# A fused attention and gated-MLP gradient kernel: DMA transfers moved between stretches, kv and W' blocks reordered, products of ones at the start, five residual sums moved to VectorE

## The chip, the cores and the metric

The kernel runs on one core of one Trainium2 chip. The metric is the device time of one execution in microseconds (us), here the median of several runs. The engines are called by their names or by those of the profile: TensorE (PE, its weight loads PEld), VectorE (DVE), ScalarE (ACT), GpSimd (POOL) and SyncE (SP), whose queue only issues DMA transfers. ScalarE and GpSimd can issue DMA transfers too.

## What is computed

The forward pass of a pre-LayerNorm block and its gradients for six of its inputs, with S = 2048 rows, D = 640, H = 32 heads of 20, F = 1728, in bf16:

```python
def A(x, wqkv, wo):                      # linear attention
    q, k, v = split_heads(x @ wqkv)
    phi = lambda t: where(t > 0, t + 1, exp(t)) + 1e-6
    pq, pk = phi(q), phi(k)
    kv = einsum("bhsd,bhse->bhde", pk, v)
    z = einsum("bhsd->bhd", pk)
    o = einsum("bhqd,bhde->bhqe", pq, kv) / (einsum("bhqd,bhd->bhq", pq, z)[..., None] + 1e-6)
    return merge_heads(o) @ wo
def B(x, w1, w3, w2):                    # gated MLP
    return (silu(x @ w1) * (x @ w3)) @ w2
h   = x + A(layernorm(x), wqkv, wo)
out = h + B(layernorm(h), w1, w3, w2)    # and the gradients for x, wqkv, wo, w1, w3, w2 from grad_out
```

## The kernel before

S is cut into 16 tiles of 128 rows (ST) or 4 chunks of 512 columns (SC), D into 5 blocks of 128 (DT), F into 14 (FT, the last of 64). Weights and activations stay in SBUF in pools that are stacked and reused; what does not fit is stored to DRAM scratch tensors (names in `_d`: pq_d, r_d, pk_d, xn_d, m_d, wT_d, kvT_d, hn_d, hh_d, gg_d) and loaded again for the backward part. The program is written in a manual schedule: the order of the calls in the source is the order of the instructions on each engine, and each engine, and each DMA-issuing queue, takes its own in that order. A wait of one instruction holds everything behind it on its engine or queue. The changes touch the forward part, which is the first 300 us or so.

**Start and k (lines 112 to 480).** x comes tile by tile, wqkv in column groups of 320 (`load_wq`, L176), both on SyncE's queue (`dma`). LayerNorm 1 takes two `BATCH_NORM_STATS` of half a row each (`Stats.part`, L147), an aggregate (L150), an addition (L151), a power on GpSimd (L152) and a normalisation (L155, on ScalarE for some tiles). For tiles 0 to 7 TensorE transposes the normalised rows (`p1_tr`, L246) and ScalarE copies them out of PSUM (L248), later tiles are transposed by DMA (L239). Then come the k products (`p1_mm`, L252), Exp and Relu on ScalarE (L269, L270) and two VectorE operations for phi (L273, L274). `m_part` accumulates M = pk^T xn for 5 row blocks (L382). The column sums of pk, Z, come along for the first blocks, `z_late` makes the rest. A list `trickle` of weight loads is issued one per tile. `ghh_chunk` (L361, L371) multiplies w2 (transposed by DMA, w2T) with a chunk of grad_out (transposed by DMA, g2T, two buffers) ahead of its use; the DMA transposes of w2T are cut in column ranges (L410), g2T is made per 512 rows (L216).

**q and M (lines 480 to 548).** q tiles (`q_tile`), the last row blocks of M with `m_end` (copies to mbs, and a DMA transpose to mT, L394), kvT blocks 0 and 1 (`kvT_block`: products at L401, then a masked copy by VectorE into bd, L203). For rows of pq the denominators are made in four steps: `r_prod` (product with Zb, on GpSimd for tiles below 6, L333), `r_red` and `r_inv` (L340 to L344), `r_scale` (L347), and `r_T`, a DMA transpose into pqT (L351).

**Hand-over (the list in `run`, lines 752 to 759).** PSUM is then shared by tags: "mm" with 4 banks, "o2" and "at" with 2 each. A step of the list is a function and its arguments: `q_late` (q tiles 10 to 15, L574, L575), `f2_mT` (the last block of mT by TensorE, L601), `f2_kv` (kvT blocks 2 to 4), `f2_wT` (W' = kv wo, L586, copied by ScalarE and VectorE to pkx, L589, and transposed by DMA to Wp, L590), then `f2_half` or `f2_at`, the residual: at = pq' Wp (L558). Where `on_pe` is true, x itself is added in PSUM by a product with the identity (L556) and ScalarE copies the sum back into x (L561). Otherwise VectorE adds x to PSUM (L563). LayerNorm 2 follows (`f2_hn`, `f2_ht`: transposes on TensorE, L633, in the first chunk). GpSimd's queue stores intermediate results: `q_out` to pq_d (L606), `f2_m_out` to m_d (L596), `r4_out` (L609), `r4b_out` (L612) and `r_out` (L355) to r_d, `f2_w_out` to wT_d (L593).

**MLP (lines 793 to 850).** For each of 4 chunks c and 14 column blocks fc: a ghh product four blocks ahead, the gate product (L361 by way of `mm5`), two sigmoids and a copy on ScalarE (L661 to L663), the up product and its copy (L669). Two blocks make a pair: VectorE runs 7 products and sums of it (L697), and three results are stored to hh_d and gg_d from SyncE's queue (L680). The tiles sig, s2, gate and up have 2 buffers, so a pair's copies wait until the stores of the pair two back have landed. `run_side` puts the residual and LayerNorm of the next chunk between, `r_steps` the denominators of tiles 6 to 15, which load pq back (`r_load`, L616), and `o2_steps` the down product of the chunk before (L721), which needs w2.

**Backward.** The rest (lines 860 to 1360) is untouched: long runs of products for the weight gradients and the input gradients.

Of the kernel before, what the change touches and what calls it, by code (L numbers as in the profile page):

```python
# [9 lines left out]
P = 128  # L10
# [45 lines left out]
def kernel(  # L56
# [116 lines left out]
    wqkv = U1.tile([P, DT, 3 * D], BF16, name="wqkv", tag="D")  # L173
    wq_v = A_wqkv.rearrange("(c p) n -> p c n", p=P)

    def load_wq(a, b):  # L176
        dma(out=wqkv[:, :, a * HD:b * HD], in_=wq_v[:, :, a * HD:b * HD])

    def load_x(a, b):
        dma(out=x_sb[:, a:b, :], in_=xS[:, a:b, :])  # L180

    load_wq(2, 3)
    load_x(1, 2)
    load_wq(3, 4)
    load_x(2, 4)
    load_x(4, 8)

    mask = cp.tile([P, DT, M_MAX, DH], BF16, name="mask")

# [38 lines left out]
    Z = cp.tile([P, DT], F32, name="Z")  # L228

    XT_DMA = 8  # L230

    def on_act(t):
        return t > XT_DMA and t % 2 == 0
# [178 lines left out]
    trickle = []  # L412

    zero_pads()
    load_g2T(0)
    load_x(8, 12)
    load_w2T(0, 2 * P)
    load_wq(0, 2)
    load_x(12, ST)
    ln1.run(x_sb, 0, 1)  # L420
    for a, b in ((0, 2 * P), (2 * P, D)):
        ln1.norm(x_sb[:, 0, a:b], x_sb[:, 0, a:b], 0)
    p1_tr(0, ((0, 2), (2, DT)))
    ln1.run(x_sb, 1, 2)
    ln1.run(x_sb, 2, 3)
    p1_norm(1)
    ln1.run(x_sb, 3, 4)
    p1_norm(2)
    trickle += [lambda: load_w2T(2 * P, 4 * P), lambda: load_wq(4, 6)]
    for c0, c1 in ((0, 2), (2, 4), (4, 5)):  # L430
        trickle += load_w13(c0, c1)
# [65 lines left out]
    q_tile(5)  # L497
    m_part(2, range(8, ST))
    m_end(2)
    phi_rest()  # L500
    m_part(3, range(5))
    z_row((2, 3, 4), big())
# [15 lines left out]
    r_prod(2)  # L518
    m_end(3)
    dmaG(out=m_v[:, 0:4, :], in_=mbs[:])  # L520
    load_w2T(8 * P, F)
    m_part(4, range(5))
    q_tile(8)
    kvT_block(1, big())
# [7 lines left out]
    q_tile(9)  # L532
    m_part(4, range(11, ST))
    m_end(4)
    phi_rest()
    r_scale(2)
    r_T(2)
    r_red(3)
    r_inv(3)
    r_prod(4)  # L540
    ps.release()
    load_x(0, 4)
    while trickle:
        trickle.pop(0)()

# [2 lines left out]
    hn, hnT, hhT = {}, {}, {}  # L548

    def f2_at(t, tag="at", halves=(0, 1)):  # L550
        on_pe = t < 2 * TPC
        for j in halves:
            at = ps.tile([P, 512], F32, name="at", tag=tag, bufs=2)
            xs = x_sb[:, t, j * HD:(j + 1) * HD]
            if on_pe:
                T.matmul(at[:, 0:HD], lhsT=ident[:], rhs=xs, start=True, stop=False)  # L556
            for c in range(DT):
                T.matmul(at[:, 0:HD], lhsT=pqT[:, c, t * P:(t + 1) * P], rhs=Wp[:, c, j * HD:(j + 1) * HD],  # L558
                         start=(c == 0 and not on_pe), stop=(c == DT - 1))
            if on_pe:  # L560
                A.copy(out=xs, in_=at[:, 0:HD])  # L561
            else:
                V.tensor_tensor(out=xs, in0=at[:, 0:HD], in1=xs, op=ALU.add)  # L563
            ln2.part(x_sb, t, j)

    def q_late(t):

        mq, rq = (p1.tile([P, D], BF16, name=n, bufs=b) for n, b in (("mq", 3), ("rq", 3)))
        q_home(t)
        for j in range(2):  # L570
            acc = ps.tile([P, 512], F32, name="mm", bufs=4)
            js = slice(j * HD, (j + 1) * HD)
            p1_half(acc[:, 0:HD], t, j * HD)
            A.activation(mq[:, js], acc[:, 0:HD], AF.Exp)  # L574
            A.activation(rq[:, js], acc[:, 0:HD], AF.Relu)  # L575

        def rest():
            V.tensor_scalar(out=mq[:], in0=mq[:], scalar1=1.0, scalar2=1e-6, op0=ALU.min, op1=ALU.add)
            V.tensor_tensor(out=pqs[t], in0=mq[:], in1=rq[:], op=ALU.add)  # L579
        held.append(rest)  # L580
# [15 lines left out]
        dmaG(out=m_v[:, 4, :], in_=mbs[:, 0, :])  # L596

    def f2_mT():
        tr = ps.tile([P, DT, P], BF16, name="trm", tag="mm", bufs=4)
        for c in range(DT):  # L600
            T.transpose(tr[:, c, :], mbs[:, 0, c * P:(c + 1) * P], ident[:])  # L601
        A.copy(out=mT[:, :, (DT - 1) * P:], in_=tr[:])
# [138 lines left out]
        A.activation(sg[:], zero[:], AF.Sigmoid)  # L741

    def f2_kv(m):
        kvT_block(m, ps.tile([P, 512], F32, name="mm", bufs=4))

    def run(*steps):
        for f, *t in steps:
# [1 line left out]

    Wp = U1.tile([P, DT, D], BF16, name="Wp", tag="MW")  # L750
    pkx.append(p1.tile([P, DT + 6, D], BF16, name="pkx", tag="pk"))
    run((q_late, 10), (f2_mT,), (phi_rest,), (q_late, 11), (f2_kv, 2), (f2_kv, 3), (f2_kv, 4), (phi_rest,), (r_scale, 3),
        (r_T, 3), (q_late, 12), (f2_wT, 0), (f2_wT, 1), (phi_rest,), (r_red, 4), (r_inv, 4), (r_prod, 5), (q_late, 13),
        (f2_wT, 2), (f2_wT, 3), (f2_wT, 4), (q_out, 8, 10), (f2_m_out,), (r4_out,), (phi_rest,), (q_late, 14), (r_scale, 4), (r_T, 4), (load_x, 4, 8),
        (mlp_ghh, 4), (phi_rest,), (q_late, 15), (f2_w_out,), (f2_half, 0, 0), (f2_half, 1, 0), (phi_rest,), (f2_half, 0, 1),
        (f2_hn, 0), (f2_half, 1, 1), (f2_hn, 1), (q_out, 10, 16), (mlp_ghh, 5), (f2_half, 2, 0),
        (f2_ht, 0), (f2_half, 2, 1), (f2_hn, 2), (sig_table,), (f2_half, 3, 0), (f2_ht, 1), (f2_half, 3, 1), (f2_hn, 3),
        (mlp_ghh, 6), (f2_ht, 2), (mlp_ghh, 7), (f2_half, 4, 0), (f2_ht, 3), (f2_half, 4, 1), (r_red, 5),
        (r_inv, 5), (r_scale, 5), (r_out, 5), (r4b_out,))
    p1.release()  # L760
    pa = pool("pa", "right")

# [35 lines left out]
    for c in range(SC):  # L798
# [8 lines left out]
        for fc in range(FT):  # L807
            mlp(c, fc, lambda: run_side(0, fc))
            drain(1)
            if o2 and not (c == SC - 1 and fc == 5):  # L810
                next(o2, None)
            run_side(1, fc)
            drain(1)
            if (c, fc) in ((0, 9), (1, 2)):
                load_x(8 + 4 * c, 12 + 4 * c)
            if c == 0 and fc in (1, 3, 5, 7):
                a, b = {1: (0, 3), 3: (3, 6), 5: (6, 10), 7: (10, 13)}[fc]
                dma(out=w2[:, a:b, :], in_=B_w2[a * P:b * P, :].rearrange("(c p) n -> p c n", p=P))
                if fc == 7:
                    dma(out=w2[0:FL, FT - 1, :], in_=B_w2[(FT - 1) * P:F, :])  # L820
            for f, t in r_steps[c].get(fc, ()):
                f(t)
            if c == 0 and fc == 3:
                dmaG(out=rows(kvT_d), in_=bd[:])
            if c == 0 and fc == 0:
                load_g2T(1)
            if fc == 3 and 0 < c < SC - 1:
                load_g2T(c + 1)
            if c == SC - 1 and fc == 0:
                g2 = U1.tile([P, ST, D], BF16, name="g2", tag="Q")  # L830
                tail = U2.tile([P, DT, P], BF16, name="w13tail", tag="g2T", bufs=2)
            if c == SC - 1 and fc in (1, 2, 5, 6):
                i = (1, 2, 5, 6).index(fc)
                dma(out=g2[:, i * TPC:(i + 1) * TPC, :], in_=goS[:, i * TPC:(i + 1) * TPC, :])
            if c == SC - 1 and fc == 8:
                dma(out=tail[:, :, 0:FL], in_=B_w1[:, F - FL:F].rearrange("(c p) f -> p c f", p=P))
                dma(out=tail[:, :, FL:P], in_=B_w3[:, 0:P - FL].rearrange("(c p) f -> p c f", p=P))
            if c == SC - 1 and fc == 9:
                wT2 = U1.tile([P, DT, D], BF16, name="wT2", tag="MW")
                dma(out=wT2[:], in_=rows(wT_d))  # L840
# [553 lines left out]
```

## Time and profile before

| | us |
|---|---|
| median of 9 runs | 845.9 (841.76 to 847.63) |
| the profiled execution's own time | 845.9 |
| its span, first to last instruction | 844.2 |
| TensorE busy | 821.0 |
| VectorE, ScalarE, GpSimd busy | 452.5, 321.0, 79.3 |
| first product on TensorE | 5.62 |
| first residual product at 92.78, first that needs Wp at | 97.33 |
| first gate product of the MLP at | 112.07 |
| DMA moved | 157.58 MB, mean 187 GB/s |

The span is one execution, taken by the hardware profiler. Its trace gives each instruction's start and duration, and for each engine what ended its idle time ("waited for"). [...] the distance from start to start is the better measure of what a product costs. PEclk is the clock that the throttle granted. The DMA share is the mean busy share of the core's 16 DMA engines[...]. "SPq" rows are issues from SyncE's queue, and their duration is the time that the issue held the queue.

### The profile page before, as it was taken

To read this page: it belongs to the slowest core of one execution; us is meant where nothing else is said; L and a number is where in the kernel's file an instruction comes from. 1 tells how busy PE (TensorE), PEld (TensorE's weight loads), DVE (VectorE), ACT (ScalarE), POOL (GpSimd) and SP (SyncE) were. 2 spreads that over 40 slices of the span, in tenths; PEclk is the share of its full clock that TensorE was granted. 3 is DMA by queue.
4 is the path that set the end of the run, shared out by engine and by line. 5 is a ranking of instruction groups with operands and counts; after the bars stand their busy time and mean duration, and the time that the engine had idled before them with its cause. 6 is when DMAs were issued, how large, how long until landed. Compare 5 with 4: busy or idle time off the path is not lost.

```text
span 844.2 us, 14063 instructions
## 1 busy us (share of the span) xinstructions
PE 821.0 (97%) x5486; PEld 522.1 (62%) x5514; DVE 452.5 (54%) x959; ACT 321.0 (38%) x608; POOL 79.3 (9%) x116
## 2 busy tenths in 40 slices
PE   6999798999999999999999999999999999999998
PEld 4676453455555555677777777777777777555554
DVE  7848587999978756600026777772582544300000
ACT  5865575765655566201111212222311333211111
POOL 2315121001001000000001111111110000000000
PEclk9999999999999999999999999999999999999999
DMA  9998869776645455799958887628798688887671
GB/s 256 303 300 169 216 186 262 231 187 166 149 116 161 135 174 167 203 259 232 270 159 201 181 193 182 147 58 150 196 247 177 133 204 177 192 206 153 155 176 37
DMA packets 329954, 157.58 MB, mean 187 GB/s; under 512 B 235232, under 2 KB 327040, under 8 KB 329888
## 3 DMA queue, kind: packets, MB, share of 16 engines
q1 hardware_dynamic: 303200, 137.43, 67.0%
q10 hardware_dynamic: 24416, 11.23, 6.1%
q0 software_dynamic: 2272, 8.03, 2.8%
q8 instruction: 43, 0.70, 0.4%
q14 instruction: 23, 0.19, 0.1%
HBM read 48.15 MB, written 51.46 MB: 118 GB/s over the span
## 4 chain that ended last, share of the span: by engine, by line
PE 86%; DMA 2%; DVE 1%; ACT 1%; issue 0%; SPq 0%; POOL 0%; DVEq 0%; ACTq 0%
PE mm L361 19%; PE job L1159 19%; PE ghn L961 14%; PE gxn L1318 8%; PE o L721 7%; PE gw L914 7%; PE gwo L1046 3%; PE dkv L1262 3%; PE gr L1018 3%; PE at L558 2%; DMA gg_d<-up 1%; DMA Wp<-pkx 1%; PE dkv L1191 1%; PE gt L893 0%; DVE pkx L579 0%
## 5 line engine op out<-in xcount | busy, mean ns | idle before, releaser
L1159 PE MATMUL job<-gb,hnN 128*128 128x432 bf16 x640 | 117.0, 346 | 0.0
L961 PEld LDWEIGHTS <-ggb 128*128 128x128 bf16 x864 | 84.5, 98 | 32.8
L1159 PEld LDWEIGHTS <-hnN 128*128 128x128 bf16 x640 | 62.6, 98 | 54.1
L361 PE MATMUL mm<-pqT,w 128*128 128x512 bf16 x399 | 94.5, 381 | 1.2 <-ACT gate L663 0.7
L361 PEld LDWEIGHTS <-w 128*128 128x128 bf16 x540 | 53.1, 98 | 64.9 <-issue 2.9
L1163 ACT CAST obs<-job 128x432 bf16<-128x432 f32 (+1 forms) x60 | 29.1, 485 | 123.1 <-PE job L1159 123.1
L721 PE MATMUL o<-w,hhT 128*128 128x320 bf16 x448 | 67.5, 299 | 0.1
L361 PE MATMUL mm<-g2T,w2T 128*128 128x512 bf16 x244 | 63.7, 383 | 3.9 <-ACT up L669 3.2
L961 PE MATMUL ghn<-w13a,ggb 128*128 128x320 bf16 x448 | 63.5, 299 | 0.0
L961 PE MATMUL ghn<-w13b,ggb 128*128 128x320 bf16 x416 | 61.4, 299 | 0.0
L721 PEld LDWEIGHTS <-hhT 128*128 128x128 bf16 x448 | 43.8, 98 | 23.6
L914 PE MATMUL gw<-g,hb 128*128 128x320 bf16 x416 | 57.0, 299 | 0.0
L914 PEld LDWEIGHTS <-hb 128*128 128x128 bf16 x416 | 40.5, 98 | 15.7
L371 ACT CAST ghh<-mm 128x512 bf16<-128x512 f32 x52 | 30.5, 586 | 52.0 <-PE mm L361 46.0
L1318 PE MATMUL gxn<-wqT,gT 128*128 128x320 bf16 x320 | 48.7, 299 | 0.0
L1026 POOL TENSOR_TENSOR sz<-Zb,g_h 128x640 f32<-128x640 bf16 x16 | 20.2, 1261 | 270.7 <-issue 163.0
L361 PEld LDWEIGHTS <-w2T 128*128 128x128 bf16 x280 | 27.4, 98 | 29.2 <-issue 4.3
L661 ACT ACTIVATE sig<-mm 128x512 bf16<-128x512 f32 x56 | 33.5, 599 | 28.0 <-PE mm L361 25.5
L252 PE MATMUL big<-wqkv,pqT 128*128 128x320 bf16 x260 | 41.8, 312 | 0.3 <-ACT rq L270 0.2
L252 PEld LDWEIGHTS <-pqT 128*128 128x128 bf16 x320 | 31.6, 101 | 15.6 <-issue 2.1
L973 ACT ACTIVATE gs<-ghn 128x640 bf16<-128x640 f32 x16 | 11.2, 703 | 77.6 <-PE ghn L961 72.7
L147 DVE BATCH_NORM_STATS2 st<-x_sb 128x6 f32<-128x320 bf16 x64 | 29.5, 486 | 18.7 <-ACT x_sb L561 15.2
(183 smaller groups left out, 1220.9 us busy)
## 6 DMA issues: line engine op xcount, KB each, us to landing
hh_d<-hhT SPq DMA_DIRECT2D x24, 256.0 KB, 2.6
gg_d<-gate SPq DMA_DIRECT2D x24, 256.0 KB, 3.0
gg_d<-up SPq DMA_DIRECT2D x24, 256.0 KB, 2.6
ggb<-gg_d SPq DMA_DIRECT2D x6, 896.0 KB, 5.7
ggb<-gg_d SPq DMA_DIRECT2D x6, 832.0 KB, 6.6
x_sb<-in_A_x_dram SPq DMA_DIRECT2D x7, 640.0 KB, 5.1
out_dram<-obs ACTq DMA_DIRECT2D x40, 108.0 KB, 3.1
ggb<-gg_d SPq DMA_DIRECT2D x2, 1728.0 KB, 14.6
```

Source lines behind the costliest of these rows:

```text
L147: V.bn_stats(out=self.st[t][:, j, :], in_=src[:, t, j * HD:(j + 1) * HD])
L252: T.matmul(acc, lhsT=pqT[:, c, t * P:(t + 1) * P], rhs=wqkv[:, c, n0:n0 + HD], start=(c == 0), stop=(c == DT - 1))
L361: T.matmul(acc[:], lhsT=w[:, c, fc * P:(fc + 1) * P], rhs=rhs[:, c, :], start=(c == 0), stop=(c == DT - 1))
L371: A.copy(out=ghh[n // 2][:, n % 2, :], in_=acc[:])
L661: A.activation(sig[:, i, :], gp[:], AF.Sigmoid)
L721: T.matmul(o2["ps"][:, 0:HD], lhsT=hhT[c][:, fc, i * P:(i + 1) * P], rhs=w2[:, fc, j * HD:(j + 1) * HD], start=(fc == 0), stop=(fc == FT - 1))
L914: T.matmul(acc[:, j, 0:HD], lhsT=hb[b][:, t, i * P:(i + 1) * P], rhs=g2[:, t, j * HD:(j + 1) * HD], start=(t == 0), stop=(t == ST - 1))
L961: T.matmul(acc[:, j, 0:HD], lhsT=ggb[t // 2][:, k, lo:lo + P], rhs=rhs[:, j * HD:(j + 1) * HD], start=(k == 0), stop=(k == NG - 1))
L1018: T.matmul(gr[t][:, j, 0:HD], lhsT=ghT[t][:, c, :], rhs=wT2[:, c, j * HD:(j + 1) * HD], start=(c == 0), stop=(c == DT - 1))
L1159: T.matmul(acc[:, 0:n], lhsT=lhs[:, t, m * P:(m + 1) * P], rhs=rhs(t), start=(t == 0), stop=(t == ST - 1))
L1163: A.copy(out=ob, in_=acc[:, 0:n])
L1318: T.matmul(acc[:, j, 0:HD], lhsT=g, rhs=wqT[:, k, j * HD:(j + 1) * HD], start=(k == 0), stop=(k == 14))
```

## The change

It moves loads and stores, reorders the steps of the hand-over, and changes where some sums are made.

- Start: the first two column groups of wqkv are issued from ScalarE's queue instead of SyncE's. x comes as tiles 1, 2, 3, then 4 to 5 and 6 to 7. The first part of w2T is issued ahead of g2T. 44 products of a tile of ones with itself (128 x 128, into a PSUM bank of tag "m" whose content is not read) stand at the head of TensorE's order. Statistics of tiles 1 to 3 are split in halves and interleaved with the normalisations.
- q and M: the second g2T is loaded after block 2 of M instead of in the MLP. The last part of w2T (columns 1024 to 1727) leaves this stretch and comes later in two parts. The first reload of x takes two tiles instead of four; `r_red` and `r_inv` of tile 3 move behind.
- Hand-over: kv blocks 2 to 4 come directly behind q tile 10, in the banks "o2" and "at". W' 0 and 1 come behind q tile 11, W' 2 to 4 behind q tile 12. The stores of m, W', pq and r on GpSimd's queue move to the residual products and behind them.
- Residual: tiles 0 to 4 are added by VectorE instead of by an identity product with a copy on ScalarE. Tiles 5 to 7 stay, tiles from 8 on were on VectorE already.
- MLP: w2 is loaded at column blocks 5, 7, 9, 11 of the first chunk instead of 1, 3, 5, 7; x tiles 8 to 11 at block 12 instead of 9; kvT is stored in the third chunk instead of the first.

```diff
 
-    def load_wq(a, b):
-        dma(out=wqkv[:, :, a * HD:b * HD], in_=wq_v[:, :, a * HD:b * HD])
+    def load_wq(a, b, q=dma):
+        q(out=wqkv[:, :, a * HD:b * HD], in_=wq_v[:, :, a * HD:b * HD])
 
 
-    load_wq(2, 3)
-    load_x(1, 2)
-    load_wq(3, 4)
-    load_x(2, 4)
-    load_x(4, 8)
+    load_wq(2, 3, A.dma_start)
+    load_wq(3, 4, A.dma_start)
+    for t in range(1, 4):
+        load_x(t, t + 1)
+    load_x(4, 6)
 
...
     XT_DMA = 8
+    WARM = 44
 
...
     zero_pads()
+    load_w2T(0, 2 * P)
+    load_x(6, 8)
     load_g2T(0)
     load_x(8, 12)
-    load_w2T(0, 2 * P)
     load_wq(0, 2)
     load_x(12, ST)
+    warm = ps.tile([P, 512], F32, name="warm", tag="m", bufs=2)
+    for _ in range(WARM):
+        T.matmul(warm[:, 0:P], lhsT=ones[:], rhs=ones[:], start=True, stop=True, skip_group_check=True)
     ln1.run(x_sb, 0, 1)
+    ln1.part(x_sb, 1, 0)
     for a, b in ((0, 2 * P), (2 * P, D)):
     p1_tr(0, ((0, 2), (2, DT)))
-    ln1.run(x_sb, 1, 2)
-    ln1.run(x_sb, 2, 3)
-    p1_norm(1)
-    ln1.run(x_sb, 3, 4)
-    p1_norm(2)
+    for t in (1, 2):
+        ln1.part(x_sb, t, 1)
+        ln1.part(x_sb, t + 1, 0)
+        p1_norm(t)
+    ln1.part(x_sb, 3, 1)
     trickle += [lambda: load_w2T(2 * P, 4 * P), lambda: load_wq(4, 6)]
...
     m_end(2)
+    load_g2T(1)
     phi_rest()
...
     dmaG(out=m_v[:, 0:4, :], in_=mbs[:])
-    load_w2T(8 * P, F)
     m_part(4, range(5))
...
     m_end(4)
+    r_prod(4)
     phi_rest()
     r_T(2)
-    r_red(3)
-    r_inv(3)
-    r_prod(4)
     ps.release()
-    load_x(0, 4)
+    load_x(0, 2)
     while trickle:
...
     def f2_at(t, tag="at", halves=(0, 1)):
-        on_pe = t < 2 * TPC
+        on_pe = TPC < t < 2 * TPC
         for j in halves:
...
 
-    def q_late(t):
+    def q_late(t, between=None):
 
...
             p1_half(acc[:, 0:HD], t, j * HD)
+            if j == 0 and between is not None:
+                between()
             A.activation(mq[:, js], acc[:, 0:HD], AF.Exp)
...
     def f2_mT():
-        tr = ps.tile([P, DT, P], BF16, name="trm", tag="mm", bufs=4)
+        tr = ps.tile([P, DT, P], BF16, name="trm", tag="at", bufs=2)
         for c in range(DT):
...
     def f2_kv(m):
-        kvT_block(m, ps.tile([P, 512], F32, name="mm", bufs=4))
+        kvT_block(m, ps.tile([P, 512], F32, name="kv", tag="at" if m == 4 else "o2", bufs=2))
 
...
     pkx.append(p1.tile([P, DT + 6, D], BF16, name="pkx", tag="pk"))
-    run((q_late, 10), (f2_mT,), (phi_rest,), (q_late, 11), (f2_kv, 2), (f2_kv, 3), (f2_kv, 4), (phi_rest,), (r_scale, 3),
-        (r_T, 3), (q_late, 12), (f2_wT, 0), (f2_wT, 1), (phi_rest,), (r_red, 4), (r_inv, 4), (r_prod, 5), (q_late, 13),
-        (f2_wT, 2), (f2_wT, 3), (f2_wT, 4), (q_out, 8, 10), (f2_m_out,), (r4_out,), (phi_rest,), (q_late, 14), (r_scale, 4), (r_T, 4), (load_x, 4, 8),
-        (mlp_ghh, 4), (phi_rest,), (q_late, 15), (f2_w_out,), (f2_half, 0, 0), (f2_half, 1, 0), (phi_rest,), (f2_half, 0, 1),
-        (f2_hn, 0), (f2_half, 1, 1), (f2_hn, 1), (q_out, 10, 16), (mlp_ghh, 5), (f2_half, 2, 0),
-        (f2_ht, 0), (f2_half, 2, 1), (f2_hn, 2), (sig_table,), (f2_half, 3, 0), (f2_ht, 1), (f2_half, 3, 1), (f2_hn, 3),
-        (mlp_ghh, 6), (f2_ht, 2), (mlp_ghh, 7), (f2_half, 4, 0), (f2_ht, 3), (f2_half, 4, 1), (r_red, 5),
-        (r_inv, 5), (r_scale, 5), (r_out, 5), (r4b_out,))
+    run((q_late, 10, f2_mT), (f2_kv, 2), (f2_kv, 3), (f2_kv, 4), (phi_rest,), (q_late, 11), (f2_wT, 0), (f2_wT, 1),
+        (phi_rest,), (q_late, 12), (f2_wT, 2), (f2_wT, 3), (f2_wT, 4), (phi_rest,), (q_late, 13),
+        (r_red, 3), (r_inv, 3), (r_scale, 3), (r_prod, 5),
+        (load_x, 2, 4), (r_T, 3), (phi_rest,), (q_late, 14), (r_red, 4), (r_inv, 4), (r_scale, 4), (r_T, 4),
+        (load_x, 4, 8), (mlp_ghh, 4), (phi_rest,), (q_late, 15), (load_w2T, 8 * P, 11 * P),
+        (f2_half, 0, 0), (f2_half, 1, 0), (phi_rest,), (f2_half, 0, 1),
+        (f2_hn, 0), (f2_half, 1, 1), (f2_hn, 1), (f2_m_out,), (mlp_ghh, 5), (f2_half, 2, 0),
+        (f2_ht, 0), (f2_half, 2, 1), (f2_hn, 2), (f2_w_out,), (sig_table,), (f2_half, 3, 0), (f2_ht, 1), (f2_half, 3, 1),
+        (f2_hn, 3), (q_out, 10, 16), (load_w2T, 11 * P, F),
+        (mlp_ghh, 6), (f2_ht, 2), (mlp_ghh, 7), (f2_half, 4, 0), (f2_ht, 3), (f2_half, 4, 1), (r4_out,), (r_red, 5),
+        (r_inv, 5), (r_scale, 5), (r_out, 5), (r4b_out,), (q_out, 8, 10))
     p1.release()
...
             drain(1)
-            if (c, fc) in ((0, 9), (1, 2)):
+            if (c, fc) in ((0, 12), (1, 2)):
                 load_x(8 + 4 * c, 12 + 4 * c)
-            if c == 0 and fc in (1, 3, 5, 7):
-                a, b = {1: (0, 3), 3: (3, 6), 5: (6, 10), 7: (10, 13)}[fc]
+            if c == 0 and fc in (5, 7, 9, 11):
+                a, b = {5: (0, 3), 7: (3, 6), 9: (6, 10), 11: (10, 13)}[fc]
                 dma(out=w2[:, a:b, :], in_=B_w2[a * P:b * P, :].rearrange("(c p) n -> p c n", p=P))
-                if fc == 7:
+                if fc == 11:
                     dma(out=w2[0:FL, FT - 1, :], in_=B_w2[(FT - 1) * P:F, :])
                 f(t)
-            if c == 0 and fc == 3:
+            if c == 2 and fc == 3:
                 dmaG(out=rows(kvT_d), in_=bd[:])
-            if c == 0 and fc == 0:
-                load_g2T(1)
             if fc == 3 and 0 < c < SC - 1:
```

## The prediction

> **What bounds the kernel now.** I read the page's busy table first, then TensorE's waits, then its timeline around each wait, and only then the other engines there.
>
> ```profile
> span 844.2 us, 14063 instructions
> PE 821.0 (97%) x5486; PEld 522.1 (62%) x5514; DVE 452.5 (54%) x959; ACT 321.0 (38%) x608; POOL 79.3 (9%) x116
> ```
>
> TensorE sets the time. There is to win only its 844.2 - 821.0 = 23.2 us of idleness, time in which busy rows run at half pace, and matmuls that are dropped. Its waits (line, releaser: total us, times, longest) say where:
>
> ```profile
> PE tr L246 <- DVE x_sb L155: 7.0, 3, 5.6
> PE at L558 <- DMA Wp<-pkx: 4.3, 1, 4.3
> PE mm L361 <- ACT up L669: 3.2, 2, 2.3
> PE mm L252 <- DVE bd L203: 1.4, 1, 1.4
> PE mm L361 <- ACT gate L663: 0.7, 1, 0.7
> ```
>
> All lie before 142 us; behind that TensorE hardly waits, so what is won before it stays won. TensorE's timeline (start, duration, instructions, idle before):
>
> ```profile
> 6.48 2.85 PE L252 MATMUL big<-wqkv,pqT 128*128 128x320 bf16 x10
> ...
> 24.55 1.52 PE L252 MATMUL big<-wqkv,pqT 128*128 128x320 bf16 x10
> ...
> 83.41 1.52 PE L252 MATMUL mm<-wqkv,pqT 128*128 128x320 bf16 x10 [1.37 <-DVE bd L203]
> ...
> 97.33 1.49 PE L558 MATMUL at<-Wp,pqT 128*128 128x320 bf16 x5 [4.26 <-DMA Wp<-pkx]
> ...
> 141.35 2.13 PE L361 MATMUL mm<-g2T,w2T 128*128 128x512 bf16 x5 [2.29 <-ACT up L669]
> 143.28 3.16 PE L361 MATMUL mm<-pqT,w 128*128 128x512 bf16 x10
> ...
> 147.91 1.24 PE L361 MATMUL mm<-g2T,w2T 128*128 128x512 bf16 x5
> ```
>
> The same ten products take 2.85 us at the start and 1.52 later; five of 512 columns take 2.13 us behind the 2.29 us wait and 1.24 six us later. So each long wait costs twice: the idleness, then about 3.7 us at half pace. What the stalls hang on, by stretch (busy us in 10; the second last column is the DMA share), SyncE's queue and ScalarE:
>
> ```profile
> 90.00:100.00 10.00, 5.69 (x30) 3.20 (x30) 2.40 (x5) 3.76 (x10) 0.88 (x1) 0.86 1.03 243
> 130.00:140.00 10.00, 8.21 (x41) 4.11 (x42) 6.16 (x10) 5.10 (x10) 0.56 (x1) 1.00 1.11 268
> ```
>
> ```profile
> 86.75 9.89 SPq L590 DMA_TRANSPOSE Wp<-pkx  x5
> 117.07 3.42 SPq L216 DMA_TRANSPOSE g2T<-in_grad_out_dram  x1
> 126.41 0.38 SPq L680 DMA_DIRECT2D gg_d<-up  x1
> ```
>
> ```profile
> 127.99 0.58 ACT L663 CAST gate<-mm 128x512 bf16<-128x512 f32 x1 [2.11 <-DMA gg_d<-gate]
> 140.72 0.58 ACT L669 CAST up<-mm 128x512 bf16<-128x512 f32 x1 [3.42 <-DMA gg_d<-up]
> ```
>
> The DMA engines are full in both stretches. Five W' transposes hold SyncE's queue for 9.89 us, two each, where other transposes of this size (pqT) issue in 1.2.
>
> **Part A, the start.** Before, VectorE waits for x at 3.21, 6.26 and 8.16 us, with 800 KB of wqkv queued between. After, x tiles 1 to 3 lead on SyncE's queue, wqkv comes through ScalarE's (two issues of some 0.4 us, idle there until 6.06), and half statistics fill the wait for GpSimd's power (0.69). Walking VectorE's order with its rows (half statistics 0.45, aggregate to power to norm 1.1, norm 0.36), norm 2 ends near 9.9 instead of 11.4 and norm 3 near 12.4 instead of 13.0, so product 1 starts near 10.2 instead of 11.98. The 44 products of ones need 44 x 0.107 us (the pitch of five transposes from 14.64 to 15.18) = 4.7 us from about 1.2, and are over by 5.9 at the latest; tr 0 came at 5.62. They would take the half-pace excess off products 0 and 1 (1.3 us each) and three transposes. But VectorE is busy 9.3 of 10 us from 10 to 30, so TensorE soon waits for norms: of some 5 us on TensorE I keep 1.6. Bounds: 3 won; 0.5 lost if the extra queue delays x tile 0 or the ones overrun.
> A rule against this is in the Trainium skill, "TensorE: Matmul & The Clock Gate", section "What's actually happening": the clock rises after a window of about 3.4 us that runs freely and is not tied to the kernel. By the row (about 3.7 us at half pace behind 141.35) the clock is up at 4.9; by the rule possibly only at 8.0, when product 0 is slow again. It would still end before tr 2, so the sum stays at 1.6.
>
> **Part B, kv and W'.** The 1.4 us wait was for a "mm" bank that VectorE's mask still held; in banks of their own kv 2 to 4 no longer hold q up. The 0.9 us before wt stays (W' 4 reuses W' 2's banks at once). Against it stands g2T 1 on SyncE's queue, ahead of the last mT transpose: 3.4 us of issue (6.4 in a full stretch), where w2T's 3.74 stood behind it. mT transposes land in 3.7 to 7.5 us, the last was issued at 73.27, and kv 2 now comes near 77.5 instead of 80.92. No row shows this wait: between 0 and 3 us; I take 0.7, as the median landing of 5.0 just misses. Gain 0.7 (1.4 to -1.6).
>
> **Part C, W' to the MLP.** Before: 92.78 (first residual product) to 112.07 (first gate product), 19.3 us. The wait disappears if W' 2 lands in time: two of its casts come one q tile (1.4 us) earlier, one more q tile (1.4) lies behind them, and GpSimd's stores (m, pq, r, W': 1.9 MB) and w2T leave the stretch. At 4 us to landing it arrives about with TensorE; I leave 1.0 of 4.3. Ten residual products (0.135 us each) leave TensorE, and five tiles' sums go to VectorE, whose rows say what that makes:
>
> ```profile
> L563 DVE TENSOR_TENSOR x_sb<-at,x_sb x16: 472/478/492, 176.6 to 280.6; 128x320 bf16<-128x320 f32 x16
> ```
>
> ```profile
> 108.00 0.45 DVE L155 TENSOR_SCALAR hn<-x_sb,ln_mv,ln_rs 128x640 bf16<-128x640 bf16 x1 [0.69 <-POOL ln_rs L152]
> ...
> 110.33 0.45 DVE L155 TENSOR_SCALAR hn<-x_sb,ln_mv,ln_rs 128x640 bf16<-128x640 bf16 x1 [0.66 <-POOL ln_rs L152]
> ```
>
> A tile took VectorE 2.33 us, power wait included; two sums at a pitch of 0.42 make it 3.2. From the first at product: two sums and statistics, phi, tile 0 to 5.5 us, tile 1 to 7.9, tile 2 to 11.1, tile 3 to 14.3; transpose, copy and tile 4's half bring the first gate product to 15.3. TensorE has only 11.1 us of work there: ten halves at 0.68, three ghh at 1.08, four transposes at 0.28. VectorE becomes the bound, with TensorE waiting 0.8 to 1.3 us four times. So 19.3 - 15.3 - 1.0 = 3.0 won (bounds 5 and 0).
> Does the clock fall in these waits? The skill, same page, "HAM oscillation", warns only of gaps over about 3.4 us. The trace is stricter (2.29 us brought half pace) but shows 1.37 us harmless at 83.41; by both these waits cost only themselves.
>
> **Part D, the MLP's first pairs.** Loss before: 4.0 us idle, plus half pace behind 141.35 (1.93 + 3.00 us by the starts, against 1.08 + 2.16) 1.7: 5.7. ScalarE waits there for stores of the pair two back. Leaving that stretch: g2T 1, kvT (800 KB), w2 by four chunks, x. Coming in ahead of it, from 7 us after at starts: GpSimd's m, W', pq (960 KB), r, pq 8 to 9, some 3 MB, and half of w2T on SyncE (about 3.4 us). 100 to 120 ran at a DMA share of 0.53 and 0.41, so it holds this, barely. The stores should then land in about 2.6 us, not 4.2 to 6.3. VectorE's lag stays (first pair product 118.45, 6.4 us behind the MLP's start; after: tile 4 to 16.7, tile 5's denominators to 18.9, tile 6's to 21.6, again 6.3), so up of pair 1 is still about 3 us late for ScalarE, of which TensorE saw under half before. I keep 2.5 of loss: gain 3.2 (bounds 5.7 and 0). w2's last parts, issued near chunk 11, have about 4 us in hand.
>
> **Sum.** 1.6 + 0.7 + 3.0 + 3.2 = 8.5. The profiled execution took 845.9 around its span of 844.2, and this is also the median: 837.4.
>
> **Rivals.**
> Case 2, chance 0.17: the stores stay late because VectorE's lag, not the DMA queue, sets them. Then D gives nothing: 840.6. For it: VectorE's 9.8 of 10 in 120 to 130; against: 2.0 to 3.4 us waits with the data already issued.
> Case 3, 0.06: the transfers only change place. kv 2 waits 3 us for mT behind g2T 1, and W' is late by as much as before; A and part of D remain: about 844.5.
> Case 4, 0.08: the hand-over runs at half pace, since VectorE's waits leave no unbroken 3.7 us. The 7.4 us of products behind the first ghh take 14.7; 3.5 of that hides in the waits, and the first MLP products lose 1.7: 5.7 more, 843.1.
> Case 5, slower, 0.09: GpSimd's stores queue behind each other. The load of pq row 8 on SyncE now waits for GpSimd's last store (before, for one made at 82), with up of pair 0 and all later stores behind it. If seven stores each take the 6 us of the rows one after another from 7.5 us after at starts, the last lands at 44 where SyncE wants it at 26: 18 us late, less 2.5 of slack, against 5.7 before: 10 us worse than before in D, 5.3 better elsewhere: 850. It decides from about 12 us late. Against it: stores issued at 82 to 86 landed in 5.8 to 7 each, so they overlap.
> The forecast itself, 0.60: 834 to 841.
>
> **Numbers.** 0.3% of 845.9 is 2.5 us, about what a measurement can tell from no change. Faster: 0.60 + 0.17 and half of case 4, 0.81; same: half of case 4 and case 3, 0.10; slower 0.09. Range: from 832.5 (A 2.5, B 1.4, C 4.5, D 5) to 844, leaving case 5 and the top of case 3 out.
>
> **What would show it.** Right: product 0 in 1.5 us; no wait on bd; at starting within 1.5 us of its predecessor; waits of TensorE for hn (trh) near 1 us; ScalarE's waits for gg_d under 2 us. Wrong: a wait of L401 for mT over 2 us, half-pace at rows, VectorE waiting for a store of pkx at hhT, or SyncE standing at the load from pq_d.

## The result and the profile after

The kernel after takes 840.86 us (median of 10 runs, 839.37 to 844.69), beside 845.34 for the kernel before (32 runs): ratio 0.9951, 95% interval 0.9939 to 0.9964, so 4.1 us of 845.3. Forecast were 837.4 us and a ratio of 0.990. The time lies in the range, and the direction is right, with half of the forecast gain. The profiled execution took 839.66 us around a span of 837.9, 6.3 less than the span before; single executions of one kernel lie some 2 us apart, so the traces tell where time went, and the medians how much it was. "At products" are those of the residual, a "half" is 320 of a tile's 640 columns, "hn" is the normalised residual, and "half pace" means that the same row takes about twice its time.

The page's busy table and TensorE's waits in the kernel after:

```profile
span 837.9 us, 14133 instructions
PE 821.0 (98%) x5520; PEld 524.2 (63%) x5548; DVE 457.2 (55%) x969; ACT 316.9 (38%) x598; POOL 79.2 (9%) x116
```

```profile
PE trh L639 <- DVE hn L155: 4.0, 2, 3.5
PE tr L247 <- DVE x_sb L155: 2.6, 3, 1.4
...
PE at L562 <- DMA pqT<-pql: 0.9, 1, 0.9
PE mm L253 <- ACT mbs L390: 0.7, 1, 0.7
PE big L253 <- DMA pqT<-x_sb: 0.6, 2, 0.4
PE bigx L402 <- DMA mT<-mbs: 0.4, 1, 0.4
PE mm L362 <- ACT gate L669: 0.2, 1, 0.2
```

Three waits of before are gone (Wp 4.3, bd 1.4, up 3.2). In their place stands one that the kernel before did not have: TensorE waits 4.0 us for normalised residuals from VectorE. Small ones for mbs, mT and pqT are new too. PE's busy time is the same 821.0, although ten products left and 44 came; it tells little here, since rows at half pace count as busy with their whole length.

Cut at three starts of TensorE (first residual product, first gate product, first output product `o`), the spans compare like this; "forecast" is the sum's parts A + B, C and D:

| stretch | before | after | change | forecast |
|---|---|---|---|---|
| up to the first residual product | 92.78 | 91.06 | -1.7 | -2.3 |
| from there to the first gate product | 19.29 | 18.65 | -0.6 | -3.0 |
| from there to the first `o` product | 54.18 | 49.61 | -4.6 | -3.2 |
| the rest | 677.95 | 678.58 | +0.6 | 0 |

So the hand-over gave a fifth of what was forecast, and the MLP's first pairs gave more. TensorE's timeline in the hand-over shows the new wait (start, duration, instructions, idle before and its releaser):

```profile
91.06 2.88 PE L562 MATMUL at<-Wp,pqT 128*128 128x320 bf16 x20
93.78 1.24 PE L362 MATMUL mm<-g2T,w2T 128*128 128x512 bf16 x5
94.86 0.84 PE L562 MATMUL at<-Wp,pqT 128*128 128x320 bf16 x5
99.19 0.71 PE L639 MATMUL trh<-ident,hn 128*128 128x128 bf16 x5 [3.48 <-DVE hn L155]
99.69 2.88 PE L562 MATMUL at<-Wp,pqT 128*128 128x320 bf16 x10
...
108.48 0.45 PE L639 MATMUL trh<-ident,hn 128*128 128x128 bf16 x5 [0.49 <-DVE hn L155]
```

The first product needs no wait for Wp: SyncE's five W' transposes held its queue for 6.53 us instead of 9.89 (`83.66 6.53 SPq L596 DMA_TRANSPOSE Wp<-pkx  x5`). But after five halves TensorE stands for 3.48 us, and the ten products behind take 2.88 us where their full pace is 1.52 (the granted clock is 0.50 from 99 to 105). VectorE's timeline says why:

```profile
89.09 0.97 DVE L348 TENSOR_TENSOR pq<-pq,rden 128x640 bf16<-128x640 bf16 x1
...
90.81 0.87 DVE L341 TENSOR_REDUCE rden<-pr 128x16 f32<-128x320 f32 x2
...
92.33 0.82 DVE L348 TENSOR_TENSOR pql<-pql,rden 128x640 bf16<-128x640 bf16 x1
...
93.90 0.48 DVE L567 TENSOR_TENSOR x_sb<-at,x_sb 128x320 bf16<-128x320 f32 x1
...
98.68 0.45 DVE L155 TENSOR_SCALAR hn<-x_sb,ln_mv,ln_rs 128x640 bf16<-128x640 bf16 x1 [0.67 <-POOL ln_rs L152]
```

There is no idle time ahead of the first sum: VectorE is at the denominators of tiles 3 and 4 (rows of L341 to L348 from 87.29 to 93.15), with phi operations of q tiles between and behind them, and starts the sum at 93.90, 2.84 us behind the product's start. By stretches of 10 us (the first numbers are the length, then busy time and count of PE, PEld, DVE, ACT, POOL; the last three are granted clock, DMA share and GB/s):

```profile
90.00:100.00 10.00, 6.52 (x47) 4.30 (x45) 8.70 (x23) 2.58 (x7) 0.56 (x1) 0.92 0.83 196
100.00:110.00 10.00, 9.19 (x51) 5.37 (x51) 7.28 (x21) 5.27 (x8) 4.04 (x6) 0.74 0.52 176
130.00:140.00 10.00, 9.72 (x51) 4.86 (x50) 7.63 (x16) 7.04 (x15) 1.51 (x2) 1.00 0.69 187
```

In 90 to 100 VectorE is now the busy one (8.70, before 2.40) and ScalarE the idle one (2.58). In 130 to 140 the DMA share has fallen from 1.11 to 0.69, and ScalarE's longest wait for a store in the first pairs is 2.27 us instead of 3.42 (`135.01 0.58 ACT L675 CAST up<-mm 128x512 bf16<-128x512 f32 x1 [2.27 <-DMA gg_d<-up]`); TensorE sees 0.2 of it.

### The profile page after: what moved, and what is told of

It is laid out like the page before. It is cut to its first block, busy times and chain, and to the rows that moved or that the text cites. A ratio compares the mean times of both kernels' runs of the same rounds, so it can differ in the third digit from the quotient of the medians.

```text
span 837.9 us, 14133 instructions
## 1 busy us (share of the span) xinstructions
PE 821.0 (98%) x5520; PEld 524.2 (63%) x5548; DVE 457.2 (55%) x969; ACT 316.9 (38%) x598; POOL 79.2 (9%) x116
## 4 chain that ended last, share of the span: by engine, by line
PE 82%; DMA 2%; DVE 1%; ACT 0%; issue 0%; ACTq 0%; DVEq 0%
PE job L1166 19%; PE mm L362 17%; PE ghn L968 14%; PE gxn L1325 8%; PE o L727 7%; PE gw L921 7%; PE gwo L1053 3%; PE gr L1025 3%; PE dkv L1269 2%; PE at L562 1%; DMA small<-m_d 1%; PE dkv L1198 1%; DVE s L703 0%; DMA gg_d<-up 0%; PE gt L900 0%
## 5 line engine op out<-in xcount | busy, mean ns | idle before, releaser
L253 PE MATMUL big<-wqkv,pqT 128*128 128x320 bf16 x260 | 39.2, 299 | 0.9 <-DMA pqT<-x_sb 0.6
L1325 PEld LDWEIGHTS <-gT 128*128 128x128 bf16 x320 | 31.3, 98 | 12.2
```

The lines of the kernel that those rows point to most:

```text
L253: T.matmul(acc, lhsT=pqT[:, c, t * P:(t + 1) * P], rhs=wqkv[:, c, n0:n0 + HD], start=(c == 0), stop=(c == DT - 1))
L1325: T.matmul(acc[:, j, 0:HD], lhsT=g, rhs=wqT[:, k, j * HD:(j + 1) * HD], start=(k == 0), stop=(k == 14))
```

## The experiments

Theory 1: VectorE bounds the hand-over; the five sums, and its late start, eat what the removed W' wait gives. Rival: the half pace behind the wait does. Beside these stand the question what the ones at the start are worth, and which of the MLP's moves carries part D. Ratios are to the kernel before, with 95% intervals, as each kernel was measured beside it.

**1. Sums back on TensorE and ScalarE.**

```diff
-        on_pe = TPC < t < 2 * TPC
+        on_pe = t < 2 * TPC
```

> The changed kernel with the five residual sums of tiles 0 to 4 back on TensorE and ScalarE. Theory 1 (VectorE bounds the hand-over: it works without a gap from 87 to 109 us, and the eight sums that stand before the fourth hn cost it 8 x 0.42 = 3.4 us): the first gate product comes 3 to 3.4 us earlier than 109.7, and the time falls by about 3 us to 838, although TensorE gets ten products (1.35 us) more. Rival (the hand-over is lost by the half pace of TensorE behind one wait, not by VectorE's work): the wait for the first hn only shrinks from 3.5 to 2.2 us, half pace stays, and the ten products make it 1 us slower, 842.

Measured: 836.93 us, ratio 0.9900 (0.9882 to 0.9919), by the ratios about 4.3 us less than after; theory 1 had said about 3. TensorE's waits for hn are 1.8 us, and the longest is

```profile
97.73 0.45 PE L639 MATMUL trh<-ident,hn 128*128 128x128 bf16 x5 [1.16 <-DVE hn L155]
98.02 0.30 PE L560 MATMUL at<-x_sb,ident 128*128 128x320 bf16 x1
98.16 0.84 PE L562 MATMUL at<-Wp,pqT 128*128 128x320 bf16 x5
```

with full pace behind it. From the first residual to the first gate product it takes 14.98 us (91.25 to 106.23) instead of 18.65, although VectorE comes from the denominators as late as in the kernel after (its first statistics start at 94.09). Ten identity products and five pairs of copies back on their engines are cheaper than five pairs of sums on VectorE by 3.7 us.

**2. The sums alone, in the kernel before.**

```diff
-        on_pe = t < 2 * TPC
+        on_pe = TPC < t < 2 * TPC
```

> The kernel before with only the five residual sums moved to VectorE. Before, VectorE stood idle for 7.3 us ahead of the first residual, so it isn't behind. Theory (the chain sum, statistics, power, norm on VectorE is longer than TensorE's own work, tile for tile 3.2 us against 2.3): the first gate product comes 1.5 to 2.5 us later than 112.1, the time is 847 to 848. Rival (the sums hide, ten products less on TensorE count): 844.

Measured: 846.45 us, ratio 1.0015 (1.0004 to 1.0027): less loss than the 847 to 848 expected, although the first gate product came 3.1 us later and not 1.5 to 2.5. VectorE was free when the first product came:

```profile
99.00 0.49 DVE L563 TENSOR_TENSOR x_sb<-at,x_sb 128x320 bf16<-128x320 f32 x1 [6.19 <-PE at L558]
```

and yet TensorE waited for hn four times, 4.2 us in all, and the stretch behind the W' wait took 17.75 us (97.47 to 115.22) where the kernel before takes 14.74 (97.33 to 112.07). So the sums cost 3.0 us there without a late start of VectorE. Of these the MLP gave back about 3: it began later, and its first `o` product came at 166.4 as in the kernel before (166.3), with waits for gate and up of 1.2 us each (0.7 and 3.2 before). So a loss in the hand-over of the kernel before was swallowed, in this trace, by the waits for stores in the MLP's first pairs; whether a gain would be, no run shows.

**3. Full pace kept through the wait.** 56 products of ones, whose result is not read, stand ahead of the first transpose of hn.

```diff
+    def keep():
+        kw = ps.tile([P, 512], F32, name="kw", tag="mm", bufs=4)
+        for _ in range(56):
+            T.matmul(kw[:, 0:P], lhsT=ones[:], rhs=ones[:], start=True, stop=True, skip_group_check=True)
...
-        (f2_hn, 0), (f2_half, 1, 1), (f2_hn, 1), (f2_m_out,), (mlp_ghh, 5), (f2_half, 2, 0),
+        (f2_hn, 0), (f2_half, 1, 1), (f2_hn, 1), (f2_m_out,), (mlp_ghh, 5), (f2_half, 2, 0), (keep,),
```

> The changed kernel with 56 products of ones, 3.1 us of TensorE, ahead of the first hn transpose, where TensorE waits 3.5 us for VectorE. They fill the wait and should keep TensorE at full pace behind it. Theory (VectorE bounds the hand-over, and TensorE's half pace behind the wait is hidden under it): the first gate product stays within 0.5 us of 109.7 and the time of 840.9. Rival (the half pace is what the hand-over lost): 2 to 2.5 us earlier, 838.5.

Measured: 843.05 us, ratio 0.9977 (0.9968 to 0.9986), 2.2 us more than after.

```profile
96.49 3.29 PE L752 MATMUL kw<-ones 128*128 128x128 bf16 x56
100.14 0.45 PE L639 MATMUL trh<-ident,hn 128*128 128x128 bf16 x5 [0.37 <-DVE hn L155]
100.43 1.52 PE L562 MATMUL at<-Wp,pqT 128*128 128x320 bf16 x10
...
106.03 0.45 PE L639 MATMUL trh<-ident,hn 128*128 128x128 bf16 x5 [1.20 <-DVE hn L155]
...
109.44 0.45 PE L639 MATMUL trh<-ident,hn 128*128 128x128 bf16 x5 [1.20 <-DVE hn L155]
```

The ten products run at full pace, and the stretch takes 18.66 us (92.01 to 110.67), as long as after's 18.65: what the clock saves, TensorE waits for VectorE in the next tiles. The same stands in the kernels of runs 4 to 8, which keep the five sums: the ten products take 1.91 to 2.72 us there, and the stretch 18.64 to 18.66 in each. The rival is refuted. The trace of run 3 lost elsewhere: 0.9 us before the first residual product (1.2 in a wait for mT), 2.5 between gate and `o`, where tile 5's first product waited 2.25 us for pqT, and 1.9 behind. Why it met these transfers later was not settled.

**4 and 5. The start.** The ones tile takes the first bank of tag "m"; in one kernel it takes one of tag "tr", in the other tile and products are left out.

```diff
-    warm = ps.tile([P, 512], F32, name="warm", tag="m", bufs=2)
+    warm = ps.tile([P, 512], F32, name="warm", tag="tr", bufs=2)
```

> The changed kernel with the products of ones in a PSUM tile of tag tr instead of m, so that the tags take the banks in the order of before. Theory (the 0.7 us wait of q tile 10 for ScalarE's copy of M block 4 comes from the tile of ones, which was the first of the pool and so turned the order of the banks): the wait disappears, q tile 10 starts at 77.7 instead of 78.4, and at most 0.7 us is won, 840.2 to 840.9. Rival (the wait comes from the reordered hand-over steps): nothing changes.

> The changed kernel without the 44 products of ones and without their tile. Theory (behind product 1 VectorE's norms bound the start, so the half pace is mostly hidden): products 0 to 2 run at half pace again, the product of tile 4 comes at most 1 us later than 18.4, and with the bank wait gone too (0.7) the time stays within 0.5 us of the changed kernel's. Rival (the ones carry the whole start, 1.6 us at 37 us): 842 or more.

Measured: 839.64 us, ratio 0.9941 (0.9918 to 0.9964) and 840.57 us, ratio 0.9944 (0.9927 to 0.9960); neither can be told from after's 0.9951. The traces are clearer. In both TensorE's 0.7 us wait for mbs is gone, and q tile 10 starts at 77.17 and 77.26 instead of 78.36. Without ones, TensorE's timeline is

```profile
7.12 2.85 PE L253 MATMUL big<-wqkv,pqT 128*128 128x320 bf16 x10
9.76 0.50 PE L247 MATMUL tr<-ident,x_sb 128*128 128x128 bf16 x5
10.45 0.45 PE L247 MATMUL tr<-ident,x_sb 128*128 128x128 bf16 x5 [0.18 <-DVE x_sb L155]
```

and product 2 comes at 13.15 us, with the ones at 13.01. The ones make product 0 shorter by 1.2 us, and TensorE then waits 1.44 us for VectorE's norm. They are worth 0.1 to 0.2 us, as run 5's theory said (within 0.5), and its rival's 1.6 us is refuted; the loads and the order of the statistics made the start earlier. Which of these two did it was not tried.

**6, 7, 8 and 9. The MLP's transfers.** All four moves undone in the kernel after; w2 and x alone undone; g2T alone undone; and, the other way round, the moves alone in the kernel before.

```diff
-    load_g2T(1)
     phi_rest()
...
-            if (c, fc) in ((0, 12), (1, 2)):
+            if (c, fc) in ((0, 9), (1, 2)):
...
-            if c == 0 and fc in (5, 7, 9, 11):
+            if c == 0 and fc in (1, 3, 5, 7):
...
-            if c == 2 and fc == 3:
+            if c == 0 and fc == 3:
                 dmaG(out=rows(kvT_d), in_=bd[:])
+            if c == 0 and fc == 0:
+                load_g2T(1)
```

> The changed kernel with the transfers of the MLP's first pairs where they were: g2T 1 at block 0, w2 at blocks 1, 3, 5, 7, x at block 9, kvT at block 3 of the first chunk. Theory (these transfers made ScalarE wait for the stores of gate and up): TensorE's waits of 2 to 4 us for ScalarE's gate and up come back with half pace behind one of them, 4.6 us slower than the changed kernel, 845; the small waits for mT and pqT before 78 us shrink by 0.4. Rival (the stores were late because of VectorE's lag or SyncE's order): less than 1.5 us slower.

> The kernel after with only the loads of w2 at fc 1, 3, 5, 7 and of x at fc 9 again; the second block of g2T and the store of kvT stay where the change put them. If w2 carries what the four moves together were worth in the kernel after (8.4 us against the runs of that call), the time is 845 to 848; if g2T and kvT carry it, 840 to 842.

> The kernel after with only the second block of g2T loaded in the MLP's first step again (w2, x and kvT stay where the change put them). In the kernel with all four MLP transfers at their old places SyncE took 5.76 us, from 116.46 to 122.22, to issue this one transposing load, between the last transpose of pqT and the first store of hh, and the four together cost 7.8 us between the first gate product and the first output product, of which w2 and x alone cost 1.1. If g2T is the carrier, this kernel takes 4 to 7 us longer than the one after there: 845 to 847. If kvT's store on GpSimd's queue carries the rest, the time stays at 841 to 842.

> The kernel before with only the moved transfers of the MLP (the second block of g2T after the third M product, w2 at fc 5 to 11 instead of 1 to 7, x at 12, kvT in block 2). Theory: in the kernel before these transfers lie over the first pairs and cost most of the 5.7 us that TensorE loses there, so 3 to 4.5 us come back: about 841.5, and the first output product comes 3 to 4.5 us earlier measured from the first gate product. Rival: they were worth 7.2 us only in the kernel after, because that one had already put its own stores of pq, r, m and W' over the same pairs; in the kernel before, which had stored most of them earlier, they are worth 1 us or less: 844 to 845.

| kernel | us | ratio (95%) | gate to `o` |
|---|---|---|---|
| after | 840.86 | 0.9951 (0.9939 to 0.9964) | 49.6 |
| after, four moves undone | 848.08 | 1.0033 (1.0020 to 1.0045) | 57.4 |
| after, w2 and x undone | 841.72 | 0.9965 (0.9951 to 0.9979) | 50.6 |
| after, g2T undone | 842.96 | 0.9978 (0.9967 to 0.9989) | 52.2 |
| before | 845.34 | 1 | 54.2 |
| before, four moves made | 842.90 | 0.9973 (0.9962 to 0.9985) | 50.2 |

Without the four moves the rest of the change makes the kernel slower than before, by 2.8 us; 845 had been expected, as fast as before. SyncE's queue in that kernel:

```profile
114.12 2.29 SPq L352 DMA_TRANSPOSE pqT<-pql  x1
116.46 5.76 SPq L216 DMA_TRANSPOSE g2T<-in_grad_out_dram  x1
122.32 0.54 SPq L685 DMA_DIRECT2D hh_d<-hhT  x1
```

and TensorE's waits:

```profile
PE at L561 <- DMA pqT<-pql: 2.9, 1, 2.9
PE mm L362 <- ACT up L674: 2.6, 1, 2.6
PE mm L362 <- ACT gate L668: 2.1, 1, 2.1
```

Issuing g2T held the queue for 5.76 us. The transpose of tile 5, issued ahead of it, landed 8.1 us after its issue instead of about 6, and the pair stores stood behind it. These waits and the half pace behind the second (five products 2.29 us instead of 1.24, ten 2.70 instead of 2.32) exceed those of after by 2.0, 2.6, 1.8 and 1.4: the 7.8 us of the table. The parts undone alone cost 1.0 and 2.6, together 3.7 of it: w2 and x are not the carrier (841.72 lies in the 840 to 842 of the other case), and g2T alone falls between its two cases (842.96, where 845 to 847 or 841 to 842 were expected). The other 4.1 are kvT's or arise only when all stand in one queue; kvT alone was not tried. In the kernel before, the four moves bring 4.0 us in the stretch they are about, within the 3 to 4.5 expected, but the ratio says 2.3 us in all, and 842.90 lies between the theory's 841.5 and the rival's 844. In that trace 1.5 us were lost again behind the first `o`, 1.1 of it where TensorE stood at 168.58 for ScalarE's copy of up, which had waited 3.7 us for a store.

**10, 11 and 12. Towards a better version.** Edits 1 and 4 together; then tile 4's denominators moved behind hn 3, and its residual into the MLP's third block (the diff leaves out the lines that place it there); then, instead of that, two waits removed: tile 2's hn in other memory, and the last part of w2T loaded later.

> The changed kernel with the five residual sums back on TensorE and the ones in the banks of tag tr, both of the edits that were faster alone. If they lie on different stretches and TensorE bounds what comes behind, they add: 836.9 less about 0.9, 836.0, ratio to before near 0.989. If the VectorE-bound hand-over swallows the earlier start: 836.9.

```diff
-        (load_x, 2, 4), (r_T, 3), (phi_rest,), (q_late, 14), (r_red, 4), (r_inv, 4), (r_scale, 4), (r_T, 4),
+        (load_x, 2, 4), (r_T, 3), (phi_rest,), (q_late, 14),
...
-        (f2_hn, 3), (q_out, 10, 16), (load_w2T, 11 * P, F),
-        (mlp_ghh, 6), (f2_ht, 2), (mlp_ghh, 7), (f2_half, 4, 0), (f2_ht, 3), (f2_half, 4, 1), (r4_out,), (r_red, 5),
+        (f2_hn, 3), (r_red, 4), (r_inv, 4), (r_scale, 4), (r_T, 4), (q_out, 10, 16), (load_w2T, 11 * P, F),
+        (mlp_ghh, 6), (f2_ht, 2), (mlp_ghh, 7), (f2_ht, 3), (r4_out,), (r_red, 5),
...
```

> As the kernel with both edits, and in addition the denominators of tile 4 (2.4 us of VectorE) moved from ahead of the residual sums to behind the fourth hn, and tile 4's residual into the MLP's third block. Theory (VectorE is still the bound of the hand-over, TensorE waits 1.8 us for hn): the waits for hn fall under 0.3 us and the first gate product comes 2 to 3 us earlier. What follows depends on the MLP: if its first pairs have room on VectorE, 834.5; if VectorE's lag there grows instead, the stores of gate and up come late again and 836 to 838 remain.

```diff
-        hn[t] = pf.tile([P, D], BF16, name="hn", bufs=2)
+        hn[t] = wqkv[:, 0, 2 * D:3 * D] if t == 2 else pf.tile([P, D], BF16, name="hn", bufs=2)
...
-        (f2_hn, 3), (q_out, 10, 16), (load_w2T, 11 * P, F),
+        (f2_hn, 3), (q_out, 10, 16),
...
-        (r_inv, 5), (r_scale, 5), (r_out, 5), (r4b_out,), (q_out, 8, 10))
+        (r_inv, 5), (r_scale, 5), (r_out, 5), (load_w2T, 11 * P, F), (r4b_out,), (q_out, 8, 10))
```

> The kernel with five sums on TensorE and ScalarE and the ones tile in the bank tag of the transposes, and two more edits: tile 2's normalised residual is put in the dead V part of wqkv, so that it does not wait for tile 0's store, and the last part of w2T is loaded behind tile 5's transpose instead of ahead of it. Theory: both waits (1.4 us of hn, 1.2 us of pqT for tile 5's first product) go, and the time falls by 1.0 to 2.0 us from 835.9, to 834 to 835. Rival: as in the kernel with tile 4's denominators late, the gain is given back at the next shared transfer, and the time stays within 0.4 us of 835.9.

Measured: 835.89 us, ratio 0.9891 (0.9873 to 0.9909); 837.51 us, ratio 0.9909 (0.9891 to 0.9926); 835.80 us, ratio 0.9896 (0.9871 to 0.9920). All three beat both kernels, the first and the third by 1.1% and 0.6%. The first met its 836.0, but 836.9, what edit 1 gives alone, lies within its interval too. The second fell into the second case of its expectation (836 to 838). With tile 4 late the first hn comes 1.1 us earlier and the first gate product 1.6 (105.25 against 106.80); but those 1.6 us are as much as tile 4's two halves cost TensorE, which now stand behind it, so nothing is shown to be won: gate to `o` takes 51.6 us instead of 49.5. TensorE's waits for hn, expected under 0.3 us, are 2.0 (2.6 in the first kernel), since VectorE in turn waits for the store of tile 0's hn, whose memory tile 2's takes:

```profile
101.16 0.45 DVE L155 TENSOR_SCALAR hn<-x_sb,ln_mv,ln_rs 128x640 bf16<-128x640 bf16 x1 [1.66 <-DMA hn_d<-hn]
```

In the third kernel the wait for pqT and the second wait for hn are gone:

```profile
PE trh L639 <- DVE hn L155: 1.2, 1, 1.2
...
PE mm L362 <- ACT up L675: 0.7, 1, 0.7
```

and `o` comes at 154.2 instead of 156.3, but the medians agree to 0.1 us. Its trace was 2.1 us shorter than that of the first kernel, its 6 runs spread from 834.07 to 837.98, and whether these two edits bring anything is not settled.

## Why the prediction was half right

**Part A was right in its sum and wrong in its reason.** Product 1 came at 10.59 us (10.2 forecast, 11.98 before), the ones ended at 6.0, product 0 took 1.68 us, and in the middle of the k stage the same ten products came 1.56 us earlier (37.11 against 38.67), where 1.6 were forecast. But the ones carried 0.1 to 0.2 of it, so that the number fits is in part luck. Nor was the clock up at 4.9 us, as the row behind 141.35 had said: 44 ones took 4.87 us, 0.11 each, to their end. And at q tile 10 the kernel after was 0.44 us behind (78.36 against 77.92): of these 2.0 us, 1.7 are waits for pqT (0.6), mT (0.4) and mbs (0.7), of which the sum had only mT's. The last came from a detail taken to cost nothing, the ones tile's PSUM tag: with another tag, or without the tile, it is gone (runs 4 and 5). That the tag shifts the order in which banks are reused is the likely reason; no row shows it.

**Part B was right in kind and too small.** From q tile 10 to the first residual product it took 12.70 us instead of 14.86: 2.2 won, where the sum had 1.4 less 0.7 for mT. The wait for bd (1.4) went as forecast; the waits ahead of wt, forecast to stay at 0.9, fell to 0.2; and kv 2 did not wait for mT. The wait for mT came earlier instead, at the first kvT block (0.4 at 68.40). It was not g2T's: the three transposes of mT were issued from 59.08 to 66.84, ahead of g2T at 66.89, and with g2T back in the MLP the wait was 1.2 (run 6) or none (run 8). TensorE was there 0.8 us earlier than before (68.0 against 68.8), while the second transpose landed only some 0.4 us earlier.

**Part C failed, at the step "From the first at product: two sums and statistics, phi, tile 0 to 5.5 us ... the first gate product to 15.3".** It took 18.65. The W' wait vanished whole, 1.0 us better than forecast. The walk missed 3.35 us, by VectorE's rows. First, 2.0 of them: it took VectorE as free when the first half's products ended (91.9), while it was at the denominators of tiles 3 and 4, which the same change had moved directly ahead, and at a phi behind them until 93.9. Second, 1.1: from the first sum to the end of hn 3 it took 14.5 us, not 13.45 (tile 0 5.2 instead of 4.65, tiles 2 and 3 3.4 each instead of 3.2). Most of this is a misread pitch: it counted 0.42 us for a sum, but from a sum's start to the next row it is 0.52, in the hand-over

```profile
104.93 0.48 DVE L567 TENSOR_TENSOR x_sb<-at,x_sb 128x320 bf16<-128x320 f32 x1
105.45 0.49 DVE L147 BATCH_NORM_STATS2 st<-x_sb 128x6 f32<-128x320 bf16 x1
105.86 0.47 DVE L567 TENSOR_TENSOR x_sb<-at,x_sb 128x320 bf16<-128x320 f32 x1
```

as in the kernel before (176.60 to 177.12); the eight sums ahead of hn 3 make 0.8 us of it. Third, 0.3 from there to the gate product.

That the sums are the cost was shown twice: 3.7 us with the late start (18.65 against 14.98), 3.0 without (17.75 against 14.74). The same four numbers put the late start at 0.9 us with the sums and 0.2 without; in the kernels without it the products behind the W' wait ran at half pace, which delayed VectorE's first sum by 0.7, so this is less than the 2.0 of the rows. No run took the denominators alone out of the way of the sums. The waits for hn were not four of 0.8 to 1.3 but one of 3.5 and one of 0.5, since TensorE had run through five halves by then. The clock fell behind the long one, which the prediction had ruled out for short ones; as run 3 shows, that cost nothing here.

That the total still lies in the range is partly luck: C gave 2.4 us less than forecast, and D 1.4 more. Of the signs named beforehand, three came out right (no wait for bd, none for W', product 0 in 1.68 us), and three spoke against it: a wait for hn of 3.5 us, half pace at the at rows, and a wait of ScalarE for gg_d above 2 us (2.27).

**Part D had the right mechanism and was too small.** 4.6 us instead of 3.2: TensorE's waits for gate and up fell to 0.2, so of the 2.5 us of loss that were kept about 1.1 stayed, 0.9 of it as a wait for pqT that had not been foreseen. That the moved transfers carry it is shown by run 9, where they alone bring 4.0 in this stretch. The case in which VectorE's lag keeps the stores late was wrong.

**Rivals.** Case 3 did not come: neither kv 2 nor the first product that needs W' waited. The hand-over ran at half pace in part (granted clock 0.74 from 100 to 110), as case 4 said, and the run that kept the pace shows that this cost nothing there. GpSimd's seven stores left between 101.07 and 114.73 and SyncE's loads of pq behind them (122.07 and 124.74) held its queue for 0.44 and 1.43 us, so case 5 was wrong; what came near it is the kernel with the MLP moves undone, where the moved stores meet the old loads and cost more than all else gains.

The 0.6 us lost behind the first `o` product, and the 2 us between the difference of the spans (6.3) and of the medians (about 4.1 to 4.5), are not located; single executions scatter by as much.

## What to carry to other kernels

Before work is moved to an engine that looks idle on average, read its timeline at the moment when the new work arrives, with everything that the same change puts ahead of it there: VectorE showed 2.40 busy us of 10 before, and 8.70 after. A wait that is removed is won only until the next engine in the chain; here TensorE's wait for a transfer of 4.3 us became one of 3.5 for VectorE. And transfers moved into a stretch and out of it belong together: half of such an exchange lost 2.8 us where the whole won 4.1.

## What the runs showed of the hardware

The length of a wait did not tell whether TensorE would run at half pace behind it. After 1.53 us of idleness (run 12, at 6.71) ten products took 2.79 us, and after 2.25 us (run 3, at 121.85) five took 1.36 instead of 0.84; yet after 2.28 us (g2T undone, at 120.28) and 2.85 us (four moves undone, at 122.23) the same five took 0.85. After 3.48 us half pace came at once in the kernel after, and about 1 us later in the kernel with the tile in "tr": ten products 2.06 us. The Trainium skill, "TensorE: Matmul & The Clock Gate", "What's actually happening", has the clock follow a window of some 3.4 us that runs freely, and fall after one idle window. That the window runs freely would fit waits of one length with both outcomes; but if a whole window must be idle, waits of 1.53 and 2.25 us could not have brought half pace, and here they did. The measurements decide: 1.53 us was enough once, and 3.48 us did not always act at once. Nor did the clock rise at a fixed time: the same 44 ones, begun at 1.13 us, took 4.87 us in the kernel after, 4.88 in run 4 and 4.05 in run 12.

A DMA transpose of the same 512 rows held SyncE's queue for 2.81 us at 66.9 in the kernel after, for 3.42 at 117.07 in the kernel before, and for 5.30 and 5.76 us when it was issued near 115 beside GpSimd's stores (runs 8 and 6). That the stores are the reason was not tried.
